# Nyström attention and two MLPs on one core: fewer products ahead of the first h, loads gated by VectorE, three f of chunk 0 split

## The chip, the cores and the metric

One NeuronCore of a Trainium2 chip runs the kernel. The metric is the device time of one execution in microseconds; the times before are three runs with a median of 875.27 us (874.94 to 875.64).

## The reference

Attention by landmarks over q, k, v of 4 batches, 8 heads, 576 positions, 64 wide, then a feed-forward layer with elu (512 to 2048 to 512), then a gated one with silu (512 to 1536 to 512). The MLP weights come as float64, and a part of the work is to turn their words into float32.

```python
q_lm = q.reshape(B, H, m, S // m, D).mean(axis=3)      # m = 32
k_lm = k.reshape(B, H, m, S // m, D).mean(axis=3)
A, Bm, C = sm(q, k_lm), sm(q_lm, k_lm), sm(q_lm, k)
Z = Bm.transpose(0, 1, 3, 2) / (norm_1(Bm) * norm_inf(Bm) + 1e-06)
for _ in range(6):
    Z = 2 * Z - Z @ Bm @ Z
x = A @ Z @ C @ v                                      # tokens 2304 x 512
h = x @ w_in
x = where(h > 0, h, exp(minimum(h, 0)) - 1) @ w_out
g = x @ w_gate
return silu(g) * (x @ w_val) @ w_out2
```

## The kernel before

The tokens are cut into chunks of 512 columns, four and a rest of 256. Attention goes batch by batch: batch 0 stands ahead of everything, batch b + 1 is woven into the MLP of chunk b. For a batch, `softmax_b`, `scores_c`, `softmax_c` and `cv` (lines 248 to 300) make the two small softmaxes and C v; `newton` (line 311) runs six steps on 32 x 32 blocks, eight heads side by side in the array, through `by_head` (line 302); `make_w` joins Z and C v; `make_u` multiplies that with blocks of w_in (i0 to i15), so that u times A gives h. `batch_a` makes A ("att"), from d, in pieces.

In a chunk, for each of 16 f, `h_mm` makes h, `elu` makes e and hl from it on ScalarE and VectorE, and two f later `y_mm` (line 521) adds hl times w_out (o0 to o15) to y. A "whole" y multiplies float32 as it is: 4 products of 512 columns. A split one takes both factors in a high and a low part in float32r: 12 products. In chunk 0, f below Y0 are whole; the later chunks are split throughout. `Weights` (line 121) prepares a weight in letters: W loads it through SP, S or s scales its upper words on ScalarE or POOL, B, D and E are three bit operations on VectorE, h, L and M split it. A load first needs a buffer ("raw") from the pool.

The order of all this is written out by hand: `PLAN` is a string of letters for the stretch ahead of chunk 0 and one for each chunk, and `play` (line 212) takes a step of the thread with that letter. Each engine and SP's queue work in that order. In PLAN[0], n is a newton step, C, c, v the C part, a and A steps of `batch_a` (with A, all of a step is on VectorE; with a, its subtraction and division are on POOL). `ps_start` (line 109) gives out the PSUM tiles ahead of the first h, and puts `BUSY[i]` products of zeros (bf16, 256 columns) into the i-th of them before its use; the list asks for 127 in all.

In a newton step of batches 0 and 1, the products with the identity add the old Z in PSUM, and ScalarE copies the tile out; from batch 2 on, VectorE adds it:

```python
if st["b"] < 2:
    if not last:
        by_head(pn, 64, rq[:, :, 0:32], rq[:, :, 0:32], 0)
    z = rq[:, :, 32:64]
    by_head(pn, 64, rq[:, :, 0:32], rq[:, :, 32:64], 32, plus=z)
```

Of the kernel before, what the change touches and what calls it, by code (L numbers as in the profile page):

```python
# [34 lines left out]
Y0, U0 = 16, 4  # L35
# [11 lines left out]
    "BEUDEWDEWSBSW,UBSWDEDE,,BDUS,qBEqD,,WSBEDWqESBlqUlWSW,BWlDWsEB,DWWWDEslB,WDESBSEW,,DbSBBsE,CDEBVDEs,DWVsn"
    "SBBW,UScEDDB,Ccn,DEEBEWs,DWnWBDSEEvBDSW,sBD,WnBW,EnWvnvSSDEBD,WBEDnEUsBE,AA,,vnAaaDEsB,Aa,hL,aAhAxD,,,E,x"
    "wu,L",
    "hUqqqL,U,l,,l,lqhLl,,bn,,Vn,hCMhM,,c,VnhChc,LhMn,,MnvhMh,,Lvvn,,UhLhLn,,v,aa,hM,A,haanAa,,M,AA,h,wMaxux,",  # L50
    "qqq,,,llU,,,l,,,q,l,b,Ccn,Un,,,VvCc,V,nU,v,vn,A,a,n,an,a,aaan,,Av,,An,Axx,xwxu",
    "U,U,WUWSs,BDWEWBD,hSE,MWhW,BDEL,hSBD,EW,hMSBDEM,WSh,WBSDEh,M,MsBDEhs,WBDE,hsW,LW,BDEBhDLE,hSMBDSW,EMWh,SB"
    ",DEMWhBS,MBWDE,shDE,WMhS,BDEM,BDW,EWhM,SB,WhX,MWsBDEhDE,,h",
    "SMSBDWSBDEhMEh,WSBDEhMWMSBDEh,MWBDEhMsB,WDEhMWSSBDEhMW,SBDEhMWBSDEhM,SBDEMWSBDEhWS,WhMBDEWhMMSBDE,WhSBDEM"
    "hS,BDEMBDEh,LWSBDhEhMM,,WSBDEhM",
# [13 lines left out]
def kernel(ctx: ExitStack, tc: tile.TileContext, qT, kT, va, vb, wi, wo, wg, wv, wo2, out):  # L69
# [232 lines left out]
    def by_head(p, width, a, b, o=0, plus=None):  # L302

        for g in range(2):
            q = slice(width * g + o, width * g + o + b.shape[2])
            for x, y in (((ident, plus),) if plus is not None else ()) + ((a, b),):
                for j in range(0, 128, 32):
                    PE.matmul(p[j:j + 32, q], lhsT=x[j:j + 32, j:j + 32] if x is ident else x[j:j + 32, g], rhs=y[j:j + 32, g],  # L308
                              start=plus is None or y is plus, stop=y is b, tile_position=(j, j), skip_group_check=True)
# [411 lines left out]
```

## Time and profile before

| what | value |
|---|---|
| median of three runs | 875.27 us |
| the profiled execution's own time | 876.06 us |
| its span, first to last instruction | 874.3 us |
| TensorE busy | 854.0 us, 98% |
| VectorE, ScalarE, POOL busy | 439.2, 323.0, 118.6 us |
| mean granted TensorE clock | 0.992 |
| DMA | 74.27 MB in 27997 packets |

The profiled execution is 0.8 us above the median, and 1.8 us of it lie outside the span. PE is TensorE (PEld its weight loads), DVE is VectorE, ACT is ScalarE, POOL is GpSimd, SP the queue from which DMAs are issued. A float32 product shows as two records of PE and two of PEld, a bf16 one as one of each.

### The profile page before, as it was taken

The numbers are of one execution on the slowest core, as the hardware profiler recorded it, in microseconds if no ns is written. First come the engines' busy times: TensorE is split into PE (matmuls) and PEld (weight loads), VectorE is DVE, ScalarE is ACT, GpSimd is POOL, SyncE is SP. The second block draws the span as 40 slices with busy tenths as digits, with TensorE's granted clock in tenths as the row PEclk, the third lists the DMA queues.
The fourth block names the chain that finished last, engine by engine and source line by source line (L and its number), as shares of the span: only waits on it lengthen the run. The fifth ranks groups of instructions, "written<-read, shape, count | busy, mean of one in ns | idle before, by whom it ended". The sixth has DMA issues, their size and how long they took to land.

```text
span 874.3 us, 13572 instructions
## 1 busy us (share of the span) xinstructions
PE 854.0 (98%) x5593; PEld 666.9 (76%) x5593; DVE 439.2 (50%) x788; ACT 323.0 (37%) x643; POOL 118.6 (14%) x111
## 2 busy tenths in 40 slices
PE   7899999999999999999999999999999999999998
PEld 5533445777787768999888888888888888888897
DVE  7598765634654367767578853222222223222332
ACT  3254436565656456666534322111111112111211
POOL 0120012334231315445100000000000000000000
PEclk9799999999999999999999999999999999999999
DMA  9990003300240025333480233000300001000100
GB/s 332 403 362 0 3 1 128 133 1 2 88 172 1 1 104 211 121 145 121 145 336 16 82 121 97 0 1 1 109 12 1 1 25 48 1 1 1 49 1 25
DMA packets 27997, 74.27 MB, mean 85 GB/s; under 512 B 3104, under 2 KB 5664, under 8 KB 27936
## 3 DMA queue, kind: packets, MB, share of 16 engines
q1 hardware_dynamic: 27936, 73.41, 23.3%
q8 instruction: 44, 0.72, 0.3%
q14 instruction: 17, 0.14, 0.1%
HBM read 59.24 MB, written 14.16 MB: 84 GB/s over the span
## 4 chain that ended last, share of the span: by engine, by line
PE 93%; ACT 3%; DMA 2%; issue 1%; DVE 1%; SPq 0%; DVEq 0%; ACTq 0%
PE ps_b L626 34%; PE ps_acc L642 17%; PE ps_acc L531 14%; PE ps_acc L526 6%; PE ps_b L501 6%; PE ps_b L491 3%; PE ps_b L531 3%; PE ps_b L495 3%; PE ps_b L407 1%; PE ps_b L245 1%; DMA raw<-wo 1%; PE ps_b L308 1%; DMA qk<-kT 1%; ACT us L192 1%; PE ps_b L294 1%
## 5 line engine op out<-in xcount | busy, mean ns | idle before, releaser
L626 PE MATMUL ps_b<-x,w 128*128 128x512 f32 (+1 forms) x1440 | 305.2, 368 | 0.0
L626 PEld LDWEIGHTS ps_b<-x,w 128*128 128x128 f32 x1440 | 252.3, 188 | 45.8
L642 PE MATMUL ps_acc<-w,hl 128*128 128x512 f32 x648 | 156.8, 389 | 0.0
L531 PE MATMUL ps_acc<-hl,w 128*128 128x512 f32 x576 | 141.0, 394 | 0.0
L642 PEld LDWEIGHTS ps_acc<-w,hl 128*128 128x128 f32 x648 | 120.9, 188 | 24.6
L531 PEld LDWEIGHTS ps_acc<-hl,w 128*128 128x128 f32 x576 | 106.0, 188 | 24.2 <-issue 2.3
L632 DVE TENSOR_TENSOR s<-s,ps_b 128x512 f32<-128x512 f32 (+1 forms) x60 | 38.0, 634 | 168.8 <-ACT s L631 168.8
L193 POOL TENSOR_TENSOR hl<-e,hl 128x512 fp32r<-128x512 f32 x64 | 80.5, 1267 | 169.9 <-ACT hl L192 161.7
L631 ACT ACTIVATE s<-ps_b 128x512 f32<-128x512 f32 (+1 forms) x60 | 33.2, 554 | 166.7 <-PE ps_b L626 166.7
L192 ACT ACTIVATE hl<-s 128x512 fp32r<-128x512 f32 (+1 forms) x60 | 35.4, 589 | 147.7 <-DVE s L633 147.7
L501 PE MATMUL ps_b<-xs,us 128*128 128x448 f32 (+3 forms) x384 | 75.1, 337 | 0.1
L510 DVE SCALAR_TENSOR_TENSOR e<-e,ps_b 128x512 f32<-128x512 f32 x64 | 39.4, 619 | 69.1 <-ACT e L508 66.7
L633 DVE TENSOR_TENSOR s<-s,ps_b 128x512 f32<-128x512 f32 (+1 forms) x60 | 38.0, 634 | 61.4 <-PE ps_b L626 60.4
L507 ACT ACTIVATE e<-ps_b 128x512 f32<-128x512 f32 x80 | 44.1, 552 | 61.5 <-PE ps_b L501 34.4
L501 PEld LDWEIGHTS ps_b<-xs,us 128*128 128x128 f32 x384 | 60.2, 189 | 1.8 <-DVE us L193 0.8
L193 DVE TENSOR_TENSOR hl<-s,hl 128x512 fp32r<-128x512 f32 (+1 forms) x60 | 38.3, 639 | 42.2 <-ACT hl L192 42.2
L526 PE MATMUL ps_acc<-hl,wf 128*128 128x512 f32 x128 | 58.0, 597 | 0.0
L168 DVE SCALAR_TENSOR_TENSOR wr<-raw,wr 128x512 int32<-128x512 int32 x68 | 50.6, 746 | 1.2
L508 ACT ACTIVATE e<-e 128x512 f32<-128x512 f32 x80 | 47.1, 589 | 2.5
L192 ACT ACTIVATE hl<-e 128x512 fp32r<-128x512 f32 x64 | 35.1, 573 | 28.9 <-DVE e L510 25.4
L526 PEld LDWEIGHTS ps_acc<-hl,wf 128*128 128x128 f32 x128 | 23.7, 190 | 28.8 <-issue 28.0
L183 ACT ACTIVATE w<-raw 128x512 fp32r<-128x512 f32 x36 | 24.1, 671 | 44.8 <-DVE raw L177 44.8
(142 smaller groups left out, 722.8 us busy)
## 6 DMA issues: line engine op xcount, KB each, us to landing
raw<-wo SPq DMA_DIRECT2D x28, 512.0 KB, 8.5
raw<-wi SPq DMA_DIRECT2D x16, 512.0 KB, 9.3
x<-x2d SPq DMA_DIRECT2D x16, 512.0 KB, 4.9
raw<-wg SPq DMA_DIRECT2D x12, 512.0 KB, 4.7
raw<-wv SPq DMA_DIRECT2D x12, 512.0 KB, 4.9
qk<-qT SPq DMA_DIRECT2D x16, 288.0 KB, 5.2
qk<-kT SPq DMA_DIRECT2D x16, 288.0 KB, 5.5
out<-o SPq DMA_DIRECT2D x18, 256.0 KB, 2.1
```

Source lines behind the costliest of these rows:

```text
L168: DVE.scalar_tensor_tensor(self.r[i], self.words(i)[1], -2 ** 31, self.r[i], ALU.bitwise_and, ALU.bitwise_or)
L192: ACT.activation(dst[:, 0], src, AF.Copy)
L193: (lo or DVE).tensor_tensor(dst[:, 1], src, dst[:, 0].bitcast(F32), ALU.subtract)
L501: PE.matmul(p[:, o:o + n], lhsT=state[b]["us", f // 4, g][:, a, cols], rhs=state["xs", c, g][:, b_, 0:n], start=i == 0, stop=i == 5)
L507: ACT.activation(e[:, 0:n], p[:, 0:n], AF.Relu, scale=-1.0)
L508: ACT.activation(e[:, 0:n], e[:, 0:n], AF.Exp, scale=-1.0)
L510: DVE.scalar_tensor_tensor(g[:, 0:n], e[:, 0:n], -1.0, p[:, 0:n], ALU.add, ALU.max)
L526: PE.matmul(acc[dc][:, 0:n], lhsT=w1.f[at1["o", f]][:, cols], rhs=g[:, 0:n], start=first, stop=last)
L531: PE.matmul(acc[dc][:, 0:n], lhsT=w[:, a, cols], rhs=g[:, b_, 0:n], start=first and i == 0 and (n == CH or dc % 2 == 0), stop=last and i = ...
L626: PE.matmul(p[:, 0:n], lhsT=w[:, a, 128 * kk:128 * kk + 128], rhs=x[kk][:, b_, 0:n], start=i == 0, stop=i == 11)
L632: DVE.tensor_tensor(s[:, 0:n], s[:, 0:n], pg[:, 0:n], ALU.mult)
L642: PE.matmul(acc[t], lhsT=u[:, a, 128 * t:128 * t + 128], rhs=w[:, b_], start=f == 0 and i == 0, stop=f == NF2 - 1 and i == 2)
```

## The change

The products of zeros become wide: float32, 512 columns, of a 128 x 128 tile of zeros with one column broadcast, and six in all are asked for. In batch 0 a newton step takes one identity product of 128 rows for all heads; batch 1 goes the way of batches 2 and 3. A new letter G writes one element of the next load's buffer on VectorE, so that this load, and all behind it on SP's queue, waits until VectorE has come to that place; it stands once in PLAN[0] and once in PLAN[1]. Y0 goes from 16 to 13, so that f = 13 to 15 of chunk 0 are split. All PLAN strings are others.

```diff
-Y0, U0 = 16, 4
+Y0, U0 = 13, 4
 PLAN = (
-    "qqqlqWlWVVlWlbSSAWAAnBBWCcCcDSnSvEAnDSaBAvAWnDnvABnAnnBDvWwEuEDSaEsB",
+    "qqqllqWSWlWVlbACacBnWWaDCsBSBnnavscsEnaaWvnVDaBAnGAvnnvWwBuDEEDAEsBSWs",
...
 BUSY = (
-    31, 0, 0, 0, 0, 0, 0, 0, 0, 0, 0, 15, 0, 15, 3, 0, 27, 0, 0, 0, 5, 4, 0, 17, 4, 0, 0, 0, 0, 0,
-    0, 0, 0, 0, 0, 0, 6,
+    3, 0, 0, 0, 0, 0, 0, 0, 0, 0, 0, 2, 0, 0, 0, 0, 0, 1, 0, 0, 0, 0, 0, 0, 0, 0, 0, 0, 0, 0,
+    0, 0, 0, 0, 0, 0, 0,
 )
...
-    zeros = const.tile([128, 256], BF16, name="zeros")
+    zeros = const.tile([128, 128], F32, name="zeros")
...
-            PE.matmul(p[:, 0:256], lhsT=zeros[:, 0:128], rhs=zeros, start=True, stop=True)
+            PE.matmul(p, lhsT=zeros, rhs=zeros[:, 0:1].to_broadcast([128, 512]), start=True, stop=True)
...
+                "G": self.gate(),
...
+        def buffer(self, i):
+            if i not in self.raw:
+                self.raw[i] = self.pools(i)[0].tile([128, 512], I64, tag="w", name="raw")
+            return self.raw[i]
+
         def load(self, i):
-            raw = self.raw[i] = self.pools(i)[0].tile([128, 512], I64, tag="w", name="raw")
-            SP.dma_start(raw, self.srcs[i])
+            SP.dma_start(self.buffer(i), self.srcs[i])
+            self.loaded = i + 1
+
+        def gate(self):
+
+            while True:
+                DVE.memset(self.buffer(self.loaded)[0:1, 0:1].bitcast(I32)[:, 0:1], 0)
+                yield
...
-            if st["b"] < 2:
+            if st["b"] == 0:
 
                 if not last:
                     by_head(pn, 64, rq[:, :, 0:32], rq[:, :, 0:32], 0)
-                z = rq[:, :, 32:64]
-                by_head(pn, 64, rq[:, :, 0:32], rq[:, :, 32:64], 32, plus=z)
+                PE.matmul(pn[:, 0:128].rearrange("p (g n) -> p g n", g=2)[:, :, 32:64], lhsT=ident, rhs=rq[:, :, 32:64],
+                          start=True, stop=False, skip_group_check=True)
+                by_head(pn, 64, rq[:, :, 0:32], rq[:, :, 32:64], 32, start=False)
```

What the new strings do to the order shows at three places. First TensorE in the second half of batch 0's Newton steps. Before, from the transposes of the second half of C (ec) to the fillers behind the next step (L308 are newton's products, nrq its tile):

```order
L284 MATMUL ps_b<-ident,ec 128x128 x4
L286 MATMUL ps_acc<-ident,ec 64x128
L308 MATMUL ps_b<-nrq 32x32 x8
L308 MATMUL ps_b<-nrq,ident 32x32 x4
L308 MATMUL ps_b<-nrq 32x32 x4
L308 MATMUL ps_b<-nrq,ident 32x32 x4
L308 MATMUL ps_b<-nrq 32x32 x4
L113 LDWEIGHTS zeros
L113 MATMUL ps_acc<-zeros 128x256
```

In the change, from the last product of zeros to the second half of C v (L319 and L362 are newton's, L307 is C v):

```order
L113 MATMUL ps_b<-zeros 128x512
L319 MATMUL ps_b<-nrq 32x32 x8
L362 MATMUL ps_b<-nrq,ident 128x2x32
L319 MATMUL ps_b<-nrq 32x32 x8
L297 MATMUL ps_acc<-ident,ec 128x128 x4
L299 MATMUL ps_b<-ident,ec 64x128
L319 MATMUL ps_acc<-nrq 32x32 x8
L362 MATMUL ps_acc<-nrq,ident 128x2x32
L319 MATMUL ps_acc<-nrq 32x32 x8
L362 MATMUL ps_b<-nrq,ident 128x2x32
L319 MATMUL ps_b<-nrq 32x32 x8
L307 MATMUL ps_acc<-v,ect 32x64 x16
```

Two identity rows of four products each became one row of one product, and no zeros stand between the fourth step and w.

Second, VectorE just ahead of nzt, which w needs. Before (L297 to L299 are C v's second half, L374 is nzt, L165, L168 and L177 the three bit operations of a weight, L471 the transposed half of att):

```order
L168 SCALAR_TENSOR_TENSOR wr<-raw,wr 128x512
L297 TENSOR_SCALAR den<-sc 128x1
L298 RECIPROCAL den<-den 128x1
L299 TENSOR_SCALAR cvn<-ps_acc,den,nrc 128x64
L374 TENSOR_TENSOR nzt<-nrq,mask_82 128x256
L177 SCALAR_TENSOR_TENSOR wf<-raw,wr 128x512 x2
L168 SCALAR_TENSOR_TENSOR wr<-raw,wr 128x512
L471 STREAM_TRANSPOSE att<-d 128x576
```

In the change (L162 is the gate's write, L310 to L312 and L386 are C v and nzt):

```order
L162 MEMSET raw 1x1
L483 STREAM_TRANSPOSE att<-d 128x576
L310 TENSOR_SCALAR den<-sc 128x1
L311 RECIPROCAL den<-den 128x1
L312 TENSOR_SCALAR cvn<-ps_acc,den,nrc 128x64
L386 TENSOR_TENSOR nzt<-nrq,mask_82 128x256
L178 TENSOR_SCALAR wr<-raw 128x512
L181 SCALAR_TENSOR_TENSOR wr<-raw,wr 128x512
L190 SCALAR_TENSOR_TENSOR wf<-raw,wr 128x512 x2
```

The gate stands ahead of the first half of att; the load that it holds is i4, the 19th on SP's queue.

Third, ScalarE from w's copy on. Before (L397 copies u, L161 scales a weight, L507 and L508 are elu):

```order
L381 ACTIVATE wt<-ps_b 128x128
L397 ACTIVATE u<-ps_acc 128x128
L397 ACTIVATE u<-ps_b 128x128
L161 ACTIVATE raw<-raw 128x512
L397 ACTIVATE u<-ps_acc 128x128
L397 ACTIVATE u<-ps_b 128x128
L161 ACTIVATE raw<-raw 128x512 x2
L507 ACTIVATE e<-ps_b 128x512
```

In the change (L409 copies u, L174 scales, L519 is elu):

```order
L393 ACTIVATE wt<-ps_b 128x128
L409 ACTIVATE u<-ps_acc 128x128
L409 ACTIVATE u<-ps_b 128x128
L174 ACTIVATE raw<-raw 128x512
L409 ACTIVATE u<-ps_acc 128x128
L409 ACTIVATE u<-ps_b 128x128
L409 ACTIVATE u<-ps_acc 128x128
L409 ACTIVATE u<-ps_b 128x128
L174 ACTIVATE raw<-raw 128x512 x2
L519 ACTIVATE e<-ps_b 128x512
```

The third block of u moved ahead of the first elu; the first scaling is of i4 and the next two are of i6 and i7, all behind the gate.

## Rows read from the trace of the kernel before

**Rows 1.** The page: busy time by engine; a DMA queue, packets, MB, share.

```profile
PE 854.0 (98%) x5593; PEld 666.9 (76%) x5593; DVE 439.2 (50%) x788; ACT 323.0 (37%) x643; POOL 118.6 (14%) x111
...
q8 instruction: 44, 0.72, 0.3%
```

**Rows 2.** Windows: us; busy us of PE, PEld, DVE, ACT, POOL; clock; DMA.

```profile
15.00:28.80 13.80, 11.14 (x267) 9.06 (x270) 13.23 (x35) 6.80 (x20) 1.85 (x2) 0.99 1.02 392
28.80:39.00 10.20, 7.72 (x187) 5.32 (x184) 3.23 (x9) 1.41 (x5) 0.00 (x0) 0.50 1.04 401
42.30:100.00 57.70, 56.19 (x346) 23.72 (x340) 52.47 (x106) 28.61 (x64) 5.29 (x7) 1.00 0.39 148
100.00:874.00 774.00, 766.34 (x4640) 620.39 (x4638) 358.33 (x613) 281.82 (x545) 109.12 (x90) 1.00 0.19 65
```

**Rows 3.** Chain of waits, 10 to 50 us: start us, us, what.

```profile
22.81 3.05 PE ps_acc L113 x27
...
26.17 1.45 issue
...
28.75 0.73 PE ps_b L308 x48
...
31.43 2.48 issue
...
35.78 1.38 PE ps_acc L294 x40
37.16 2.91 PE ps_b L113 x17
```

**Rows 4.** Timeline of TensorE: start us, us, engine, line, op, tiles, count.

```profile
40.90 0.29 PE L392 MATMUL ps_acc<-wf,wt 64*32 64x128 f32 x1
...
42.32 1.98 PE L491 MATMUL ps_b<-att,u 128*128 128x512 f32 x4
...
48.62 3.70 PE L526 MATMUL ps_acc<-hl,wf 128*128 128x512 f32 x8
...
92.23 0.33 PE L308 MATMUL ps_b<-nrq 32*32 32x32 f32 x16
...
92.78 0.66 PE L284 MATMUL ps_b<-ident,ec 128*128 128x128 f32 x4
...
177.49 0.43 PE L308 MATMUL ps_b<-nrq 32*32 32x64 f32 x16
177.85 1.17 PE L245 MATMUL ps_b<-qk,lc 64*32 64x288 f32 x16
```

**Rows 5.** Timeline of VectorE; in brackets its idle time before, and what ended it.

```profile
18.48 0.41 DVE L342 SCALAR_TENSOR_TENSOR nrq<-ps_acc,nnrc,eye 128x32 f32<-128x32 f32 x2
...
37.23 0.34 DVE L299 TENSOR_SCALAR cvn<-ps_acc,den,nrc 128x64 f32<-128x64 f32 x1 [6.93 <-PE ps_acc L294]
37.49 0.41 DVE L374 TENSOR_TENSOR nzt<-nrq,mask 128x256 f32<-128x256 f32 x1
```

**Rows 6.** Timeline of POOL.

```profile
21.64 1.20 POOL L456 TENSOR_TENSOR d<-d,amx 128x576 f32<-128x576 f32 x1 [19.74 <-DVE amx L455]
```

**Rows 7.** Timeline of ScalarE.

```profile
22.87 1.30 ACT L458 ACTIVATE d<-d 128x576 f32<-128x576 f32 x2 [0.65 <-POOL d L456]
24.07 0.26 ACT L360 ACTIVATE nrq<-ps_b 128x128 f32<-128x128 f32 x1
...
40.48 0.28 ACT L381 ACTIVATE wt<-ps_b 128x128 f32<-128x128 f32 x1 [4.35 <-PE ps_b L378]
```

**Rows 8.** Line 150, the loads of weights: from issue to landing.

```profile
DMA to landing us min/median/max: 3.4/8.0/11.5
```

**Rows 9.** Chain of waits of the whole span: a whole y, a split one.

```profile
54.04 3.43 PE ps_acc L526 x8
...
156.84 2.75 PE ps_acc L531 x12
```

More of the change, by code (lines that the diff above doesn't have):

```diff
@@ L45 @@
 PLAN = (
-    "qqqlqWlWVVlWlbSSAWAAnBBWCcCcDSnSvEAnDSaBAvAWnDnvABnAnnBDvWwEuEDSaEsB",
[L47 to L55, printed above, removed]
+    "qqqllqWSWlWVlbACacBnWWaDCsBSBnnavscsEnaaWvnVDaBAnGAvnnvWwBuDEEDAEsBSWs",
+    "DEWBUWDEUBSS,DED,B,WUqESB,DEGDE,q,lqWsWBBSDEDWqBUWEl,WsBllSWDEWBDW,WDESB,DEsBWWSBWS,EDEBSWD,bDEBE,WSDSWVB"
+    "VD,B,DSBSUWCEcDnWEEBE,SCcnWDBD,SEB,SsWBEDnESBSDWWvD,E,S,nvBDEnvEBDE,BU,haa,Dn,ESBDLvEaAha,A,ahnM,Aaa,n,,w"
+    "xxu,L,hh",
+    "hMULq,UM,lq,,lV,qqll,,ChLbn,,n,hhhM,,cnLM,Cc,Vnh,h,vhM,L,vnv,nLhL,hULhLn,,,ava,,Aa,anAA,Aa,A,,,wxxu,",
+    "q,,,lqUq,q,l,V,,lUl,,,bVn,Cc,n,,,nv,Cc,U,,n,A,a,n,vaAnA,v,AA,AAvn,,,n,Axwxxxu,",
+    "U,U,WWWS,WUBsWDBEhD,SE,LWBWh,WDEL,hsB,,sLDEh,WsBDM,BSEhLS,,BDEhDEs,WBDE,hhLWS,,BDEhBDLW,EhMSBMD,EhMWW,,SB"
+    "DEhssMB,,DEWM,WBSWWDES,BS,WW,DE,,,BDBDE,,hWESXhhhWBDELM",
+    "WWhhMSLMsBDSBDEhMSE,BBSDMEWhM,DEBhMhMDEh,sBDEhWMSSBDWS,EhBDEhWWMBDEM,hMSsBDMEWBWSDEshM,WhMWBDEhMSBDE,WhSB"
+    "DBEhLMWs,DEBDh,SBDEhEMhMM,,WSBDEhL",
 )
 BUSY = (
-    31, 0, 0, 0, 0, 0, 0, 0, 0, 0, 0, 15, 0, 15, 3, 0, 27, 0, 0, 0, 5, 4, 0, 17, 4, 0, 0, 0, 0, 0,
-    0, 0, 0, 0, 0, 0, 6,
+    3, 0, 0, 0, 0, 0, 0, 0, 0, 0, 0, 2, 0, 0, 0, 0, 0, 1, 0, 0, 0, 0, 0, 0, 0, 0, 0, 0, 0, 0,
+    0, 0, 0, 0, 0, 0, 0,
 )
@@ L129, in __init__ @@
             self.splits = splits
+            self.loaded = 0
             n = range(len(srcs))
@@ L300, in cv, with by_head @@
         yield
-    def by_head(p, width, a, b, o=0, plus=None):
+    def by_head(p, width, a, b, o=0, start=True):
         for g in range(2):
[L305 to L309, printed above, removed]
+            for j in range(0, 128, 32):
+                PE.matmul(p[j:j + 32, width * g + o:width * g + o + b.shape[2]], lhsT=a[j:j + 32, g], rhs=b[j:j + 32, g],
+                          start=start, stop=True, tile_position=(j, j), skip_group_check=True)
     def newton(st, ps):
@@ L357, in newton @@
             rn = at.tile([128, 2, 64], F32, tag="nrq", bufs=2, name="nrq")
-            if st["b"] < 2:
+            if st["b"] == 0:
                 o = 32 if last else 0
```

## The prediction

> **What bounds the kernel now.** I read the page first. TensorE is busy for 854.0 us of a span of 874.3, and it runs 5593 matmul records and as many weight loads [rows 1]. So the time falls only if TensorE gets less to do or stands less. Then the windows, to see where it stands. From 100 us to the end it idles 774.0 − 766.34 = 7.7 us, and from 42.3 to 100 it idles 1.5 us [rows 2]. Ahead of that, 854.0 − 56.19 − 766.34 = 31.5 us of 42.3 are busy, so some 11 are idle, and much of the busy time is filler. The loss is at the front, so the front's chain of waits comes next [rows 3]: the filler of 27 products takes 3.05 us of the chain and that of 17 takes 2.91, and twice TensorE waits for nothing that the profile shows, 1.45 and 2.48 us, each time in the middle of a Newton step. The timeline of TensorE then gives the marks by which I count: the first product of u at 40.90, the first h at 42.32, the first y at 48.62 [rows 4]. From there on the other engines have to keep ahead of it; VectorE is the nearest to failing, with 52.47 us of work in the 57.7 us from 42.3 to 100 [rows 2].
>
> The two unnamed waits I read as instructions that have not arrived. Queue 8 moved 44 packets of instructions [rows 1], 2 × 5593 / 44 = 254 instructions each, and both waits fall where the DMA share is 1.02 to 1.04 [rows 2], that is, where no DMA engine has room. The Trainium skill's page "Runtime: NRT & Kernel Launch", section "Instruction fetch mechanics", also gives 256 instructions to a block; it says besides that crossing into a new block is mostly hidden. By that sentence the waits would be something else and would stay; that case is a rival below, worked out from the two rows.
>
> **The change part by part.**
>
> *Fewer instructions ahead of the first h.* A small float32 product is two weight loads and two matmuls, a filler one of each. Six steps with 8 identity products give 192 instructions; as one wide product each, 24. The fillers go from 127 × 2 = 254 to 6 × 4 = 24. Some 400 instructions are gone, about one and a half packets, and loads pause besides. I take both waits as gone: −3.9 us of the chain, bounds 0 and −3.9. The wide product (128 by 64 columns) has no row; below it is nothing, above it stand the four records of w's two products, 0.4 us at half clock; the eight that it replaces cost about 0.2. I book nothing.
>
> *Newton's chain, walked through the new orders.* The first step begins when VectorE has written rq, which ended at 18.9 [rows 5]; one weight row moves behind it, so about 18.5. The third copy now waits for both exponentials of d, and both subtractions ahead of them are on POOL, one behind the other. Before, one was there: 1.20 us from 21.64 [rows 6], the two exponentials began at 22.87 and the second step's copy ended at 24.33 [rows 7]. Now the second subtraction ends near 24.05, its exponential (0.65) near 24.7, and the copy at 25.0, but this is the third step's copy. From there no filler of length is left. Three steps at 0.73 us at half clock [rows 3], a copy of 0.26 each [rows 7] and some 0.1 us for a handover make 3.3 us, to 28.3; the last products of v 1.38 [rows 3], to 29.7; cvn and nzt 0.34 + 0.41 [rows 5], less their overlap, to about 30.3; w's products and their copy (0.28, [rows 7]) to 31.0. The first product of u thus starts near 31.0 where it started at 40.90, 9.9 us earlier: 3.9 of unnamed waits, some 6 of filler and waiting behind it.
>
> *The gate.* The write of one element costs VectorE 0.1 to 0.2 us, twice. It stands behind both sums of d and both divisions, which wait for the exponential at 24.7: about 27.9. Every load behind it on SP waits, batch 1's q and k too. A weight load lands 3.4 us after issue at the least [rows 8]: i4 near 31.4, with the 8.0 median of a full queue as the other bound; the queue is empty then, so I take 3.4. ScalarE scales i4 ahead of the copies of u's second block, so these end near 32.9, the third block follows, and the first h starts at about 33.4 instead of 42.32. The second gate stands behind the third hl, near 45.6; o3 lands near 49 and its y is wanted near 58. That wait is covered by the products of f = 0 to 2.
>
> *The clock.* It was 0.50 (1.2 GHz) from 28.8 to 39.0 and 1.00 (2.4 GHz) afterwards, so the first h found it up [rows 2], after the last filler. Now TensorE comes to h from short products with gaps between. Three h of four records each at 3.43 / 8 us [rows 9] and the last of u are about 5.4 us at full clock. Bounds of the loss: nothing, if it is up at once; 2.6 us if it stays down for 5.1 us, as long as it did between the end of the second unnamed wait at 33.9 and 39.0. That row is the nearest thing, and part of that stretch was loose work, so I take 2.0. The first y: 33.4 + 5.4 + 2.0 = 40.8, against 48.62: **−7.8 us**. ScalarE scales i6 and i7 before the first e; at 392 GB/s [rows 2] they land 2.6 and 3.9 us after i4, so e begins near 36 and hl of f = 0 is there some 2 us later, in time. The Trainium skill, page "TensorE: Matmul & The Clock Gate", section "What's actually happening", says the throttled state is the default and activity releases it, which speaks against taking the filler out; the trace agrees that the clock was down while TensorE stood and up after the filler, and the rule's own outcome is the slow rival below.
>
> *Three f split.* A whole y is 3.43 us of TensorE, a split one 2.75 [rows 9]: 3 × 0.68 = **−2.0 us**. The splitting of those three weights is only earlier; the three extra splits of g cost ScalarE and POOL about a us each, under TensorE's stream, since they have two f of lead.
>
> *Newton of batch 1.* A step took 92.78 − 92.23 = 0.55 us; one without identity takes 177.85 − 177.49 = 0.36 [rows 4]. Six steps: **−1.1 us**. VectorE gains six short additions.
>
> *VectorE.* Its second transposed attention block is done about 6.7 us earlier, TensorE wants things 7.8 us earlier, and it had 5.2 us idle from 42.3 to 100 [rows 2]. Most of the lag fits; I book **+0.5 us**, bounds 0 and +3.
>
> Sum: −7.8 − 2.0 − 1.1 + 0.5 = −10.4. The profiled execution took 876.06 us, so 865.7; the median before is 0.8 below it, so **864.9 us**.
>
> **The rivals.**
>
> *The waits stay.* If the two unnamed waits are not fetching, or fetching still collides with loads, 3.9 us come back: 868.8. For it: the 18 loads ahead of the gate, 6.7 MB, keep the DMA engines full to about 21 at 392 GB/s [rows 2]. Against: counted along the order (four instructions to a small float32 product, two to a filler), the waits came some 700 and 970 instructions in; now the last Newton step and the first y lie there, when those loads have landed. Chance 0.13.
>
> *VectorE becomes the bound.* In chunk 0 it must prepare 26 weights and take part in batch 1's attention; if its lag of 1 us and the 4 us of paused loads can't be absorbed, TensorE waits for u's blocks or hl, 2 to 4 us: 867 to 869. For it: 91% busy. Against: hl has two f of lead, some 5 us. Chance 0.18.
>
> *The clock stays down (slower than before).* Without filler TensorE could run chunk 0 at 1.2 GHz. Each us at half clock loses half a us. My sum allows 4 us from 33.4; to eat the other 10.4 it must stay down 21 us more, to about 58. Staying to 65 gives about 879. For it: the clock was down for 10 us while TensorE was 76% busy [rows 2]. Against: wide products without a gap come from 33.4, and with such work it never fell after 39. Chance 0.04.
>
> *The front doesn't move.* If the chain from 18 to 31 is held by a wait that I have not seen (a late v, POOL's scalings ahead of the subtractions), only the last two terms remain, −3.1: 872.2, and a little more slowness makes it the same. Chance 0.06.
>
> **How the numbers follow.** My forecast has 0.59 and its own range is 862 to 868; the low end is a clock that is up at once and no lag of VectorE. The range for 8 in 10, 861.5 to 870.5, takes in the first two rivals and leaves out the last two. A measurement here can tell 0.2%, 1.75 us, from no change: the median must fall below 873.5. All cases but the last two do: faster 0.91; the same 0.05 (part of the last rival); slower 0.04.
>
> **What would show it.** First u product near 31, first h near 33.4, first y near 41; no unnamed wait of over 0.5 us on TensorE before the first h; a granted clock of 0.5 around 25 to 37 and 1.0 after; no DMA from about 22 to 28; y of f = 13 to 15 at 2.75 us; batch 1's steps at 0.36. Wrong if the first y is later than 44, if TensorE idles over 3 us between the first y and 100 us, or if the clock is down beyond 45.

## The result, and the profile after

The changed kernel takes **864.6 us** in the median of four runs (863.06 to 866.53), against 875.14 for the kernel before (874.94 to 875.64): 0.988 of it, 95% interval 0.986 to 0.990. The prediction was 864.9. The profiled run took 864.63 with a span of 862.8. So the time came out as forecast, but the two halves of the sum did not: the front gave less than booked and the rest gave more.

The page of the changed kernel, to set against [rows 1]:

```profile
PE 847.2 (98%) x5236; PEld 659.7 (76%) x5236; DVE 434.3 (50%) x791; ACT 323.2 (37%) x641; POOL 131.9 (15%) x123
...
PEclk7899999999999999999999999999999999999999
...
q8 instruction: 41, 0.67, 0.3%
```

TensorE has 6.8 us less work, and three packets of instructions fewer came. Its windows (columns as in [rows 2]), cut where the granted clock changes:

```profile
10.30:20.40 10.10, 9.39 (x102) 4.14 (x104) 8.15 (x29) 2.98 (x11) 1.99 (x3) 0.50 0.98 376
20.50:34.10 13.60, 10.71 (x312) 7.27 (x302) 12.91 (x30) 5.94 (x19) 3.33 (x3) 1.00 0.29 92
34.20:40.90 6.70, 5.73 (x22) 2.57 (x23) 5.06 (x9) 3.92 (x9) 1.16 (x1) 0.50 1.03 405
45.00:100.00 55.00, 54.23 (x301) 23.65 (x299) 50.34 (x110) 27.20 (x60) 3.30 (x4) 1.00 0.61 233
100.00:862.00 762.00, 757.03 (x4469) 618.10 (x4468) 348.21 (x601) 279.23 (x537) 120.95 (x101) 1.00 0.19 66
```

By these rows the clock was at 1.2 GHz twice: for ten us while the scores of C and the first Newton products ran, and for seven while the last of u and the first three h ran. TensorE's timeline has the marks that answer to [rows 4]:

```profile
18.36 1.91 PE L113 MATMUL ps_b<-zeros 128*128 128x512 f32 x2
20.21 0.41 PE L319 MATMUL ps_b<-nrq 32*32 32x32 f32 x16
...
32.30 0.29 PE L404 MATMUL ps_acc<-wf,wt 64*32 64x128 f32 x1 [0.37 <-ACT wt L393]
...
35.17 0.42 PE L404 MATMUL ps_acc<-wf,wt 64*32 64x128 f32 x1 [1.39 <-ACT u L409]
...
35.95 7.89 PE L503 MATMUL ps_b<-att,u 128*128 128x512 f32 x12
...
44.14 3.70 PE L538 MATMUL ps_acc<-hl,wf 128*128 128x512 f32 x8
...
86.60 0.42 PE L319 MATMUL ps_b<-nrq 32*32 32x64 f32 x16
86.96 0.66 PE L297 MATMUL ps_b<-ident,ec 128*128 128x128 f32 x4
```

And the chain of waits, 10 to 50 us, shows what held the first h, where [rows 3] had fillers and waits without a name:

```profile
19.43 0.41 DVE nrq L353 x2
...
29.30 4.97 DMA raw<-wi
34.30 0.67 ACT raw L174
34.96 0.17 ACT u L409
```

First u product 32.30 (before 40.90), first h 35.95 (42.32), first y 44.14 (48.62). Between the first y and the end of TensorE's work lay 870.49 − 48.62 = 821.9 us before and 858.98 − 44.14 = 814.8 now. So of the 11.5 us between the two spans **4.5 came from ahead of the first y and 7.0 from behind it**; 7.8 and 2.6 were forecast. These two lengths are what the experiments are judged by. For the table, the half clock is read from short windows of the profile, its ends to about half a us; "rest" is first y to the end of TensorE's work; all are of the profiled run, whose own time stands last.

| kernel | first h | first y | rest | at 1.2 GHz | us |
|---|---|---|---|---|---|
| before | 42.32 | 48.62 | 821.9 | 12–15, 29–39 | 876.06 |
| changed | 35.95 | 44.14 | 814.8 | 10–20.5, 34–41 | 864.63 |
| no gate | 35.55 | 42.57 | 815.2 | 11–21, 35–38 | 863.49 |
| i4 ahead of the gate | 39.66 | 47.88 | 814.9 | 11–14, 21–44.5 | 868.37 |
| no zeros | 39.07 | 46.56 | 815.6 | to 15, 19–42.5 | 867.80 |
| one zero more, at w | 40.78 | 48.87 | 815.1 | 11.5–14.5, 22–45.5 | 869.61 |
| Y0 = 16 | 36.08 | 43.84 | 816.9 | 9.5–16, 33.5–40 | 866.35 |
| identity in batch 1 | 36.47 | 44.33 | 817.6 | 10–20, 34–40.5 | 867.66 |
| before, no zeros | 36.52 | 45.09 | 821.6 | to 14, 17.5–41.5 | 872.31 |
| old order of chunk 2 | 35.51 | 44.00 | 817.8 | 10.5–20.5, 34–41 | 867.45 |
| zeros at more places | 33.92 | 39.64 | 815.2 | never after 8 | 860.47 |
| the same, no gate | 36.89 | 42.61 | 815.2 | 28–35 | 863.43 |
| the same, i4 behind | 36.24 | 41.97 | 814.9 | 27.5–34.5 | 862.52 |
| small identity | 35.15 | 43.58 | 815.7 | 10–20, 30.5–40.5 | 864.88 |

The clock at the very start needs care: until some 5 to 8 us (14 and 15 us in the two kernels without zeros) the profile reads 1.00, but the products run at half that pace. TensorE's timeline of the kernel with zeros at more places has the same twelve records of zeros before and after:

```profile
1.91 5.49 PE L113 MATMUL ps_acc<-zeros 128*128 128x256 f32 x12 [1.91 <-DVE zeros L107]
...
15.50 2.88 PE L113 MATMUL ps_b<-zeros 128*128 128x256 f32 x12
```

And 16 records of scores have a pitch of 0.96 us at 12.9 in the run without zeros, 0.49 at 12.4 here. So I count the start as 1.2 GHz; the table says so only where it reaches beyond 8 us.

In every row the time is first y + rest + 5.6, to 0.1 us. Where the code of the chunks is the changed kernel's, the rest stays within 814.8 to 815.7, whatever the front does; so one profile's difference in the rest is good to about 0.9 us. Of the 7.0 us, 4.1 are less work of TensorE behind the first y (816.2 to 812.1 us busy) and 2.9 less idle time (5.7 to 2.7).

### The profile page after: what moved, and what is told of

It is laid out like the page before. It is cut to its first block, busy times and chain, and to the rows that moved or that the text cites. A ratio compares the mean times of both kernels' runs of the same rounds, so it can differ in the third digit from the quotient of the medians.

```text
span 862.8 us, 12887 instructions
## 1 busy us (share of the span) xinstructions
PE 847.2 (98%) x5236; PEld 659.7 (76%) x5236; DVE 434.3 (50%) x791; ACT 323.2 (37%) x641; POOL 131.9 (15%) x123
## 4 chain that ended last, share of the span: by engine, by line
PE 95%; DVE 2%; DMA 1%; ACT 1%; issue 0%; SPq 0%; DVEq 0%
PE ps_b L638 34%; PE ps_acc L654 17%; PE ps_acc L543 17%; PE ps_b L513 7%; PE ps_acc L538 5%; PE ps_b L503 4%; PE ps_b L507 3%; PE ps_b L543 3%; PE ps_b L419 2%; PE ps_b L258 1%; PE ps_b L319 1%; DMA qk<-kT 1%; DMA raw<-wi 1%; PE ps_b L307 1%; DVE lc L244 0%; PE ps_b L297 0%
## 5 line engine op out<-in xcount | busy, mean ns | idle before, releaser
L543 PE MATMUL ps_acc<-hl,w 128*128 128x512 f32 x612 | 151.1, 396 | 0.0
L543 PEld LDWEIGHTS ps_acc<-hl,w 128*128 128x128 f32 x612 | 112.3, 188 | 28.2 <-issue 3.3
L206 POOL TENSOR_TENSOR hl<-e,hl 128x512 fp32r<-128x512 f32 (+1 forms) x67 | 83.2, 1252 | 179.0 <-ACT hl L205 167.6
L522 DVE SCALAR_TENSOR_TENSOR e<-e,ps_b 128x512 f32<-128x512 f32 (+1 forms) x67 | 41.4, 621 | 89.4 <-ACT e L520 85.7
L519 ACT ACTIVATE e<-ps_b 128x512 f32<-128x512 f32 x80 | 44.1, 552 | 66.5 <-PE ps_b L513 39.6
L181 DVE SCALAR_TENSOR_TENSOR wr<-raw,wr 128x512 int32<-128x512 int32 x68 | 52.4, 773 | 1.1
L205 ACT ACTIVATE hl<-e 128x512 fp32r<-128x512 f32 (+1 forms) x67 | 37.0, 575 | 30.9 <-DVE e L522 29.0
L538 PE MATMUL ps_acc<-hl,wf 128*128 128x512 f32 x104 | 47.3, 597 | 0.0
L196 ACT ACTIVATE w<-raw 128x512 fp32r<-128x512 f32 x36 | 23.8, 670 | 42.4 <-DVE raw L190 40.5
L538 PEld LDWEIGHTS ps_acc<-hl,wf 128*128 128x128 f32 x104 | 19.3, 190 | 23.2 <-issue 22.3
```

Of the source, the lines that this page charges most:

```text
L181: DVE.scalar_tensor_tensor(self.r[i], self.words(i)[1], -2 ** 31, self.r[i], ALU.bitwise_and, ALU.bitwise_or)
L205: ACT.activation(dst[:, 0], src, AF.Copy)
L206: (lo or DVE).tensor_tensor(dst[:, 1], src, dst[:, 0].bitcast(F32), ALU.subtract)
L519: ACT.activation(e[:, 0:n], p[:, 0:n], AF.Relu, scale=-1.0)
L522: DVE.scalar_tensor_tensor(g[:, 0:n], e[:, 0:n], -1.0, p[:, 0:n], ALU.add, ALU.max)
L538: PE.matmul(acc[dc][:, 0:n], lhsT=w1.f[at1["o", f]][:, cols], rhs=g[:, 0:n], start=first, stop=last)
```

## Experiments on the front

**No gate.**

```diff
-    "qqqllqWSWlWVlbACacBnWWaDCsBSBnnavscsEnaaWvnVDaBAnGAvnnvWwBuDEEDAEsBSWs",
-    "DEWBUWDEUBSS,DED,B,WUqESB,DEGDE,q,lqWsWBBSDEDWqBUWEl,WsBllSWDEWBDW,WDESB,DEsBWWSBWS,EDEBSWD,bDEBE,WSDSWVB"
+    "qqqllqWSWlWVlbACacBnWWaDCsBSBnnavscsEnaaWvnVDaBAnAvnnvWwBuDEEDAEsBSWs",
+    "DEWBUWDEUBSS,DED,B,WUqESB,DEDE,q,lqWsWBBSDEDWqBUWEl,WsBllSWDEWBDW,WDESB,DEsBWWSBWS,EDEBSWD,bDEBE,WSDSWVB"
```

> The changed kernel with both of VectorE's gates taken out of the order, so that no load waits; all products as in the changed kernel. Theory 1 (the unnamed waits of 1.45 and 2.48 us in the kernel before came from blocks of instructions that were fetched while the DMA engines were full, and it is the pause of the loads that removed them): an unnamed wait of 1 to 2.5 us comes back on TensorE between 24 and 36 us, the wait of 1.39 us for the scaling of i4 goes, and the first y starts between 44 and 46 (changed kernel: 44.14); time 864 to 867. Theory 2 (the smaller number of instructions alone removed them, because the block that the chain needs is fetched earlier): no unnamed wait over 0.5 us, i4 has landed by 25, the first h starts near 34.5 and the first y near 42.7; time 862.5 to 864. In both VectorE does the same work but for two short writes.

Measured: 865.34 us (863.49 to 867.37), 0.9885 of before (0.986 to 0.991). TensorE has no wait without a name between 18 and 40 us, though the loads never paused (DMA share 1.02 to 1.04 in each of the windows that cover 15 to 45). First y 42.57. That is theory 2 for the waits and the first y (the median lies above its range), and in this kernel the gate is not what removed the waits. The time is no better than that of the changed kernel within its spread.

**The kernel before, without zeros.**

```diff
 BUSY = (
-    31, 0, 0, 0, 0, 0, 0, 0, 0, 0, 0, 15, 0, 15, 3, 0, 27, 0, 0, 0, 5, 4, 0, 17, 4, 0, 0, 0, 0, 0,
-    0, 0, 0, 0, 0, 0, 6,
 )
```

> The kernel before, without any of its 127 small products of zeros, with nothing else changed. Theory 1 (the filler's only work is to hold the clock up, and without it the 192 identity instructions a step remain, with loads running): TensorE has the clock at 0.5 from some 20 us to 40 or later, the chain of small products takes longer, unnamed waits of 1 to 2.5 us stay since the loads still fill the DMA engines; first h 40 to 43, first y 48 to 50; time 873 to 877. Theory 2 (the filler is what makes the front long and also what pushes the instruction blocks over the full queue; taking it out is the whole gain of the front): no unnamed wait over 0.5, first y at 43 to 46; time 869 to 872. The stretch from the first y to the end of TensorE's work stays at 821.9 in both.

(The 192 identity instructions are those of all six steps, 32 a step.) Measured: 872.32 us (871.19 to 872.77), 0.9963 of before (0.995 to 0.998): 3 us faster, between the theories. TensorE ran at 1.2 GHz to 14 and from 17.5 to 41.5, and still the first y came 3.5 us earlier than with 127 fillers. The waits without a name shrank from 1.45 + 2.48 to these two in TensorE's timeline:

```profile
22.39 0.28 PE L305 MATMUL ps_b<-nrq,ident 32*32 32x32 f32 x5 [0.36 <-issue]
...
34.92 0.37 PE L389 MATMUL ps_acc<-wf,wt 64*32 64x128 f32 x1 [0.61 <-issue]
```

With 254 instructions fewer 3.0 of 3.9 us are gone while the loads run on at a DMA share of 1.03; with the identity's instructions gone as well (no gate, above) all are. (Its chain also runs at half clock, which leaves a late block more time; the run without gate has full clock from 21 to 35.) So with few enough instructions ahead of the first h these waits are gone, and the pause of the loads is not needed for it. That what is late are blocks of instructions stays an inference: queue 8 moved 44, 43 and 41 packets in the three kernels. The Trainium skill, page "Runtime: NRT & Kernel Launch", section "Instruction fetch mechanics", says that crossing into a new block is mostly hidden. If the waits are such crossings, the traces agree for the changed kernel (none is seen), while the kernel before has 3.9 us that were not hidden.

**Small identity.** The opposite edit in the changed kernel: the identity of batch 0's steps as eight products again.

```diff
-                PE.matmul(pn[:, 0:128].rearrange("p (g n) -> p g n", g=2)[:, :, 32:64], lhsT=ident, rhs=rq[:, :, 32:64],
-                          start=True, stop=False, skip_group_check=True)
+                for g in range(2):
+                    for j in range(0, 128, 32):
+                        PE.matmul(pn[j:j + 32, 64 * g + 32:64 * g + 64], lhsT=ident[j:j + 32, j:j + 32], rhs=rq[j:j + 32, g, 32:64],
+                                  start=True, stop=False, tile_position=(j, j), skip_group_check=True)
```

> The changed kernel with the identity of batch 0's six Newton steps again as eight small products (32 by 32), which brings back 168 of TensorE's instructions ahead of the first h; zeros, gate and order stay. Judged by the unnamed waits and by the first y (44.14 in the changed kernel, 42.6 in the run without gate). Theory 1 (it is the number of instructions that the blocks have to bring, and the first gate frees the DMA engines for them): no unnamed wait over 0.5 us; a step is 0.05 to 0.25 us shorter at full clock, since eight small products have a pitch of 0.1 to 0.2 where the wide one has 0.37; first y 0.3 to 1.2 us earlier where the clock runs as in the changed kernel. Theory 2 (the wide product was needed): an unnamed wait of 0.6 to 2.5 us between 20 and 36 us.

The output of this kernel is another than the reference's (I take it because all identity products of a step begin their sums ahead of all others, so that z of batch 0 differs; no run tests it). So it stands for instructions and waits alone, which are those described. Measured: 865.06 us (two runs), 0.988 of before (0.986 to 0.990). No wait without a name, first h 0.8 us earlier than in the changed kernel, first y 0.6. So theory 1: the wide product was not needed for that. The small ones gain little: the first u product starts 0.3 us earlier (32.03), since TensorE waits 1.51 us for VectorE's nzt (0.89 in the changed kernel); the rest of the 0.8 goes with i4, which landed after 3.5 us here and 4.97 there.

This run also limits what was shown of the pause. The traces have 1231 records of TensorE (products and weight loads) ahead of the first h in the kernel before, 989 without its zeros, 1045 here, 877 in the changed kernel with or without gate. Here, with the loads paused (DMA share 0.02 from 20.5 to 29), 1045 records run without an unnamed wait; with loads running and in the old order, 989 still have 0.97 us of them. At that number the pause, or the order, may count; no run takes the two apart.

**No zeros in the changed kernel.**

```diff
 BUSY = (
-    3, 0, 0, 0, 0, 0, 0, 0, 0, 0, 0, 2, 0, 0, 0, 0, 0, 1, 0, 0, 0, 0, 0, 0, 0, 0, 0, 0, 0, 0,
-    0, 0, 0, 0, 0, 0, 0,
 )
```

> The changed kernel without any of its six wide products of zeros. Theory 1 (those six hold the clock up from 20.5 to 34.1, and without them Newton's steps and w run at 1.2 GHz): granted clock 0.5 from some 10 us to 37 or later, first h 1 to 3 us later than 35.95, the three h of f = 0 to 2 at half clock for longer than in the changed kernel, first y 46 to 48; time 866 to 868.5. Theory 2 (they only fill time, and the chain of copies between the steps sets the pace): the first h comes 0 to 1.5 us earlier, first y 43 to 44.5; time 863 to 865.

Measured: 867.35 us (866.49 to 867.80), 0.990 of before (0.9885 to 0.991); first h 39.07, first y 46.56. Theory 1 in the times. The clock rises for a short stretch at 15, falls at 19 while TensorE stands for nrq (3.27 us, to 19.79), and stays at 1.2 GHz until 42.5; the three h take 7.2 us, not more than in the changed kernel.

**i4 ahead of the gate, and one zero more.** Two edits that should each take something off the front.

```diff
-    "qqqllqWSWlWVlbACacBnWWaDCsBSBnnavscsEnaaWvnVDaBAnGAvnnvWwBuDEEDAEsBSWs",
+    "qqqllqWSWlWVlbACacBnWWaDCsBSBnnavscsEnaaWvnVDaBAnWGAvnnvwBuDEEDAEsBSWs",
```

> The changed kernel with the load of i4 moved ahead of the first gate, so that the gate holds back i5 and what follows. Theory 1 (after the fix of the chain it is i4's landing, 4.97 us behind the gate where 3.4 was booked, that sets the first h): i4 lands before 26, the wait of 1.39 us on TensorE for the scaled u goes, the first h starts near 34.5 instead of 35.95 and the first y 1.4 to 2.5 us earlier than 44.14; time 862 to 863.5. Theory 2 (the copies of u and the scaling queue on ScalarE is what h waits for): the first h moves by less than 0.5 us, and the time stays within 1 us of the changed kernel's 864.6.

```diff
-    3, 0, 0, 0, 0, 0, 0, 0, 0, 0, 0, 2, 0, 0, 0, 0, 0, 1, 0, 0, 0, 0, 0, 0, 0, 0, 0, 0, 0, 0,
+    3, 0, 0, 0, 0, 0, 0, 0, 0, 0, 0, 2, 0, 0, 0, 0, 0, 1, 0, 0, 0, 0, 0, 1, 0, 0, 0, 0, 0, 0,
```

> The changed kernel with one more wide product of zeros, ahead of the products of w, where TensorE stands for about 0.9 us. Theory 1 (the fall of the clock to 0.5 at 34.1 comes from the thin work between 29 and 34, and costs 2.7 us, the three h taking 7.8 us where twelve records at full clock take 5.15): the clock stays at 1.0 through the three h, they take 5.2 to 6, the first y is 1.5 to 2.7 us earlier than 44.14; time 862 to 863.5. Theory 2 (one product is too little, or what decides is the wait of 1.39 us ahead of the first h): the clock falls as before, the first y stays within 0.6 us; time 864 to 865.5.

With i4 ahead, both theories missed; with one zero more, two runs lie in theory 1's range of time and two above both. This is the finding. With i4 ahead, all four runs took 867.08 to 868.97 (0.991, 0.9896 to 0.9925): TensorE did not wait for i4, but was at 1.2 GHz from 21 to 44.5. With one zero more the four runs took **862.77, 862.80, 869.58 and 869.61** (0.989, 0.9845 to 0.993), at a mean granted clock of 0.995 to 0.996 in the first two and 0.982 to 0.984 in the others. Its profile is of a long one; the short ones have no trace:

```profile
11.40:14.50 3.10, 3.10 (x52) 1.78 (x60) 1.76 (x6) 1.20 (x5) 0.66 (x1) 0.51 1.05 405
14.70:21.60 6.90, 4.89 (x83) 2.62 (x67) 6.43 (x25) 2.05 (x7) 1.28 (x2) 0.99 0.83 309
22.00:45.00 23.00, 21.34 (x290) 12.03 (x285) 16.20 (x34) 8.28 (x26) 3.97 (x4) 0.50 0.51 193
```

(windows, columns as before). In the changed kernel's own profile the clock was down while the zeros ahead of the first step ran, took 3.7 us over four records, and came up at 20.5 for the small products. Here it was up for them, they were done in 2 us, TensorE stood for nrq for 1.17 us (in the run with i4 ahead for 1.35), and the clock fell for all that followed. I infer that the stands at 7 to 11 and 15 to 20 us decide which stretch the slow clock hits; the next run tests it by filling them. Between the runs of this one kernel the difference is 6.8 us.

**Zeros at more places.** So zeros of half the width were put where TensorE stands: after each of the first three pairs of landmarks' products, ahead of nbt's, more of them ahead of the first step, and at w and the first u; with i4 ahead of the gate.

```diff
-    3, 0, 0, 0, 0, 0, 0, 0, 0, 0, 0, 2, 0, 0, 0, 0, 0, 1, 0, 0, 0, 0, 0, 0, 0, 0, 0, 0, 0, 0,
+    6, 0, 0, 0, 0, 0, 0, 0, 0, 0, 1, 6, 0, 0, 0, 0, 0, 2, 0, 0, 0, 0, 0, 2, 1, 0, 0, 0, 0, 0,
...
-            PE.matmul(p, lhsT=zeros, rhs=zeros[:, 0:1].to_broadcast([128, 512]), start=True, stop=True)
+            PE.matmul(p[:, 0:256], lhsT=zeros, rhs=zeros[:, 0:1].to_broadcast([128, 256]), start=True, stop=True)
...
+            if st["b"] == 0 and pr < 3:
+                PE.matmul(pb[1][:, 256:512], lhsT=zeros, rhs=zeros[:, 0:1].to_broadcast([128, 256]), start=True, stop=True,
+                          skip_group_check=True)
```

> The changed kernel with the load of i4 ahead of the first gate, and with the zeros as products of half the width (256 columns) at more places: six ahead of everything as before in work, one after each of the first three pairs of landmarks' products, one ahead of the first of Newton's products, six (in place of four) ahead of the first step, two at w, one at the first u. Theory 1 (the front of the changed kernel swings by up to 5 us, first y at 42.6 to 48.9 in the runs so far, because the waits at 7 to 11, 15 to 16 and 18 to 20 us let the clock fall at a moment that differs from run to run; filled, it stays up): granted clock 1.0 from some 12 us to the end of the front or at half for at most one stretch of 3.5 us, first h at 34 to 35, first y at 39.8 to 42, time 860 to 862.5, and the runs lie within 2.5 us of each other. Theory 2 (such filler cannot hold the clock, or at half clock it delays the chain itself): first y at 44 or later, runs from 863 to 870.

Measured: **860.68 us** (860.03 to 863.39), 0.984 of before (0.982 to 0.985). Theory 1, but for the spread, which one of five runs makes 3.4 us. Its windows and marks on TensorE:

```profile
10.00:20.00 10.00, 8.63 (x142) 5.82 (x142) 9.12 (x32) 3.27 (x12) 1.73 (x3) 1.00 1.03 393
20.00:31.00 11.00, 9.64 (x256) 7.01 (x255) 10.32 (x24) 4.97 (x17) 3.58 (x4) 1.00 0.32 105
31.00:45.00 14.00, 13.18 (x91) 5.82 (x92) 13.83 (x27) 7.88 (x19) 1.67 (x1) 1.00 0.64 238
```

```profile
18.62 0.42 PE L322 MATMUL ps_b<-nrq 32*32 32x32 f32 x16 [0.24 <-DVE nrq L356]
...
33.92 5.42 PE L506 MATMUL ps_b<-att,u 128*128 128x512 f32 x12
...
39.64 3.70 PE L541 MATMUL ps_acc<-hl,wf 128*128 128x512 f32 x8
```

The first step starts 1.6 us earlier than in the changed kernel, and the twelve records of h take 5.4 us, not 7.9. This is faster than both kernels. The Trainium skill, page "TensorE: Matmul & The Clock Gate", section "What's actually happening", says that the throttled state is the default and activity releases it. The trace agrees in that the first zeros run at half pace and the clock is up from 8 us on, behind them.

Two variants of it. First without either gate, with i4 in its place of the changed kernel:

> The same as the run with zeros at more places, but with both of VectorE's gates taken out and i4 where the changed kernel has it, so that no load ever waits. Theory 1 (with so few instructions TensorE never waits for a block, full DMA engines or not, and the gate gives nothing): no unnamed wait over 0.5 us, first y within 0.6 us of the kernel with the gate wherever the clock ran alike, and the median within 1.5 us of it. Theory 2 (the gate is worth something: without it a block of instructions or a later load is late): an unnamed wait of over 0.5 us in the front, or waits for weights after the first y; 1.5 to 4 us slower.

Measured: 859.99 us (859.70 to 863.43), 0.983 of before (0.981 to 0.985), no wait without a name from 20 to 40 us: theory 1 on the gate (the first y, 42.61, can't be compared, since the clock ran differently). The profiled run was the longest of the four; its clock fell at 28 for seven us, when TensorE had stood 0.76 and 0.46 us for nrq. Those two stands alone don't decide it, for TensorE's timeline of the run with the gate has them too, and there the clock stayed up:

```profile
24.98 0.33 PE L322 MATMUL ps_b<-nrq 32*32 32x32 f32 x16 [0.76 <-ACT nrq L375]
...
27.96 0.43 PE L365 MATMUL ps_b<-nrq,ident 128*128 128x64 f32 x2 [0.46 <-ACT nrq L375]
```

Then with the gate, i4 behind it:

> The kernel with zeros at more places (860.68 us, first y 39.64), but with the load of i4 back behind the first gate, where the changed kernel has it; so the two differ in the place of one load. Theory 1 (behind the gate the landing of i4 is what the first h waits for, whatever the clock does): a wait of 1 to 3 us on TensorE for u, since the chain before it is some 1.5 us earlier than in the changed kernel while the gate moves less; first h 35 to 36.5 in place of 33.92, first y 41 to 42, or 43 to 44 where that wait lets the clock fall; time 862 to 864.5. Theory 2 (the clock was all, i4 only waits because the clock makes the rest late): first h within 0.6 us of 33.92, time within 0.8 us of 860.7.

Measured: 861.98 us (859.89 to 862.56), 0.984 of before (0.9825 to 0.985). The 1.3 us between the medians fit theory 1, but the spreads overlap, and in the profiled run the slow clock (27.5 to 34.5) delayed u so far that nothing waited for i4. Of the runs at a mean clock of 0.999 to 1.000, those with i4 behind took 859.89, 861.97, 861.98 and 862.56, those with i4 ahead 860.03 to 860.77; so its place seems to be worth 1 to 2 us in most runs, but none of these slower ones was traced, and through what it acts stays open.

Of the fourteen runs of these three kernels, eleven have a mean clock of 0.999 or 1.000 (859.70 to 862.56 us) and three one of 0.996 (862.52 to 863.43). So the zeros hold the clock in most runs, not in all.

## Experiments on the rest

**Y0 back to 16.**

```diff
-Y0, U0 = 13, 4
+Y0, U0 = 16, 4
```

> The changed kernel with Y0 back at 16, so that the last three f of chunk 0 run whole instead of split; the order is otherwise that of the change. Judged by the stretch from the first y to the end of TensorE's work, which took 814.8 us in the changed kernel's profile (44.14 to 858.98) and 814.2 to 815.2 in the runs before this one, while the front moves with the clock. Theory 1 (the three split f give 3 x 0.68 = 2.0 us, the term of the prediction): the stretch gets 2.0 us longer, 816.8. Theory 2 (part of the -7.0 us that this stretch lost is more than that, since the split work also moves what follows): 3 us or more. Theory 3 (the splits cost elsewhere what they give): under 1 us.

(By the table, the runs ahead of this one had a rest of 814.9 to 815.6.) Measured: rest 816.95, 2.1 us longer: theory 1, though the rest alone spreads by 0.9. (Time 866.35 us, 864.17 to 870.97, 0.990 of before, 0.987 to 0.994; the front's clock makes the spread.)

**Identity in batch 1.**

```diff
-            if st["b"] == 0:
+            if st["b"] < 2:
```

(in both places)

> The changed kernel with the wide identity product and the copies on ScalarE also in the six Newton steps of batch 1, as batch 0 has them, in place of VectorE's six additions. Judged by the stretch from the first y to the end of TensorE's work, 814.8 us in the changed kernel. Theory 1 (the identity's cost on TensorE is all there is): a wide product has a pitch of 0.37 us at full clock, six of them make the stretch 2.2 us longer; the eight small ones of the kernel before cost 1.1. Theory 2 (VectorE's additions there delay the weights it prepares, and without them TensorE waits less): 1 us or less.

Measured: rest 817.63, 2.8 us longer; 868.79 us (two runs), 0.9925 of before (0.990 to 0.9945). Theory 1, with 0.6 more than booked, because a step now has two sets of products of 32 columns where it had one of 64. TensorE's timeline has one of its steps:

```profile
96.95 0.33 PE L319 MATMUL ps_b<-nrq 32*32 32x32 f32 x16
97.20 0.43 PE L362 MATMUL ps_b<-nrq,ident 128*128 128x64 f32 x2
97.57 0.33 PE L319 MATMUL ps_b<-nrq 32*32 32x32 f32 x16
97.83 0.65 PE L307 MATMUL ps_b<-v,ect 128*32 128x64 f32 x32
```

The wide product has a pitch of 0.37 us, and the whole step takes 97.83 − 96.95 = 0.88. With eight small products a step of the kernel before takes 0.55, without identity 0.36 [rows 4]. So the wide one adds 0.52 to a step and the eight small ones 0.19: it has fewer instructions and takes longer. No run puts the eight small ones back into batch 1.

**The old order of chunk 2.**

```diff
-    "q,,,lqUq,q,l,V,,lUl,,,bVn,Cc,n,,,nv,Cc,U,,n,A,a,n,vaAnA,v,AA,AAvn,,,n,Axwxxxu,",
+    "qqq,,,llU,,,l,,,q,l,b,Ccn,Un,,,VvCc,V,nU,v,vn,A,a,n,an,a,aaan,,Av,,An,Axx,xwxu",
```

> The changed kernel with the order of work of chunk 2 (one string of the plan, in which batch 3's landmarks, Newton steps, w and first u are placed) put back to that of the kernel before. Judged by the stretch from the first y to the end of TensorE's work, 814.8 us in the changed kernel. Theory 1 (part of what that stretch gained, and which the prediction did not name, is that w and the first u of batch 3 now stand a whole y earlier, so that VectorE's split of u is covered): waits for us on VectorE of 0.5 to 1.1 us come back at the end of chunk 2, near 306 to 320, 1.8 to 2.6 us in all, 816.6 to 817.4. Theory 2 (those waits went because VectorE has less work or lags less): under 0.7 us.

Measured: rest 817.78, **2.9 us longer**, a little above theory 1; 867.57 us (two runs), 0.991 of before (0.989 to 0.993). The waits are back, the same as in the kernel before. TensorE's timeline at the end of chunk 2, of the kernel before:

```profile
320.08 0.92 PE L495 MATMUL ps_b<-att,u 128*128 128x192 f32 x4 [0.60 <-DVE us L193]
...
323.66 1.68 PE L407 MATMUL ps_b<-wf,wt 64*32 64x512 f32 x16 [1.08 <-DVE us L193]
```

and of this run:

```profile
311.22 0.92 PE L507 MATMUL ps_b<-att,u 128*128 128x192 f32 x4 [0.60 <-DVE us L206]
...
314.81 1.68 PE L419 MATMUL ps_b<-wf,wt 64*32 64x512 f32 x16 [1.08 <-DVE us L206]
```

In the changed kernel a y of 12 records stands between the first and the second part of u there:

```profile
305.43 1.10 PE L419 MATMUL ps_b<-wf,wt 64*32 64x256 f32 x32 [0.38 <-ACT wt L393]
306.46 3.01 PE L543 MATMUL ps_acc<-hl,w 128*128 128x512 f32 x12
309.40 1.09 PE L419 MATMUL ps_b<-wf,wt 64*32 64x512 f32 x16
```

Under those 3 us VectorE splits u (307.25 to 308.54). Of the 2.9 us, the two waits make 1.7, and the 16 records of u behind the longer one, 1.68 us where the changed kernel takes 1.09, another 0.6; the rest was not taken apart. In the plan it is the ending: w and the first u's part stand one unit ahead of the last (`Axwxxxu,` for `Axx,xwxu`; other letters of the string differ too, and the swap took them along).

## Why the prediction was right, and where not

The total was right because two errors met, and that was luck. The sum had −7.8 for the front and −2.6 for the rest; the runs showed −4.5 and −7.0. Of the 3.3 us that the front fell short, 2.55 stand ahead of the first h (35.95 for 33.4) and 0.8 behind it.

- **"Both waits as gone: −3.9 us of the chain."** They are gone, and the reason given first, the count of instructions, is enough for that in the changed kernel; the pause of the loads, given beside it, is not needed there. The rival that the waits stay fell. ("Some 400 instructions are gone": the traces have 354 records fewer.)
- **"So about 18.5", the first Newton step.** It began at 20.21. The scores of C ran at 1.2 GHz from 10 us on, so VectorE wrote rq only at 19.43 to 19.84, and the zeros ahead of the step, at half clock too, ran to 20.27. The prediction looked at the clock from 25 us on only, though the kernel before also had a short fall at 12. With zeros at more places and the clock up, the step began at 18.62 and the third copy ended at 24.94, where 25.0 was forecast; so the walk along the chain was right to there but for the clock. Of the 1.7 us, 1.3 came through: first u product 32.30 for 31.0, gate at 29.21 for 27.9.
- **"The queue is empty then, so I take 3.4", i4's landing.** It took 4.97 us in the profiled run. The wait that this made, 1.39 us ahead of the last part of u, is the longest on TensorE between 11 us and the first h. What made it long is open. The loads that follow it on the queue do not explain it: with the same loads behind the same gate, i4 landed after 3.5 to 3.7 us in five traces (no zeros, one zero more, small identity, old order of chunk 2, zeros at more places with i4 behind) and after 5.3 and 5.5 in two (Y0 = 16, identity in batch 1). The bounds, 3.4 and 8.0, held it.
- **"I take 2.0", the half clock in the three h.** 7.9 us for twelve records where 5.4 are enough, 2.5 lost; the bound of 2.6 was nearer. The place was right, the stretch (34 to 41) later and shorter than the 25 to 37 forecast: in this run the clock was up from 20.5 to 34. Without zeros it was down from 19 to 42.5, but with the same zeros and i4 ahead it was down from 21 to 44.5, so that too was partly luck. The whole front thus ended at 44.14; by its own mark, "wrong if the first y is later than 44", this part of the forecast failed.
- **"Three f split: −2.0."** Measured alone, 2.1, to within 0.9.
- **"Newton of batch 1: −1.1."** A step takes 86.96 − 86.60 = 0.36 us, as forecast; the sum over six steps was not measured alone.
- **"+0.5 us" for VectorE's lag.** None shows: from 45 to 100 TensorE idles 0.8 us, nearly all of it one wait of 0.77 for u, which the kernel before has too. This is where the failed step of the rest lies: the prediction looked in the new order for what could be late, and put at nothing the waits of the old one that could go. They were in the 7.7 us that it had read from the window of 100 to the end, of which 3.5 lie behind the last product (870.49) and 4.2 between products. The new end of chunk 2 gives 2.9. With 2.0 and 1.1 that makes 6.0 of 7.0. The other 1.0 is hardly more than the spread of the rest; this wait for u in TensorE's timeline, which only the kernel before has, would be most of it, but no run took it apart:

```profile
83.60 1.98 PE L491 MATMUL ps_b<-att,u 128*128 128x512 f32 x4 [0.74 <-ACT u L413]
```

- **The clock stays down** (the slow rival). Part of it is real: the front has half-clock stretches that differ from trace to trace, and runs of one kernel lie up to 6.8 us apart, the slower ones at the lower mean clock. Its price, 14 us, was far off: once the wide products of h and y run without a gap, the clock came up in every profiled run, at 45.5 at the latest.

## What to carry to other kernels

Judge a change by stretches that do not touch each other: here the time is first y + rest, and a median that agrees with the forecast hid errors of 3.3 and 4.4 us of opposite sign. Try filler for the clock where TensorE would stand anyway, and in a few wide products, and judge it by several runs: here 127 small ones cost 3 us net; six wide ones gave some 2.7 against none and left the rest to chance; more of them in the gaps gave 4 us more and a full clock in eleven of fourteen runs. Width and place of the filler were not tested apart. When an order is replaced, list the waits of the old order first, each one by place, and ask of each whether the new order covers it.

## What was not expected of the hardware

The same kernel on the same chip took 862.8 twice and 869.6 twice, with nothing on record but the mean granted clock to tell them apart (0.995 or 0.996, and 0.982 or 0.984). Zeros that ran at half clock (3.8 us, in the changed kernel) went with full clock for the chain behind them, zeros that ran at full clock (2.0 us, with i4 ahead and with one zero more) with half clock; that the gap they left made it fall is an inference. One wide identity product of 128 rows adds 0.52 us to a Newton step, eight of 32 rows together 0.19. The first load of 512 KB behind a pause of the queue landed after 3.5 to 5.5 us with the same loads behind it, where the shortest landing of the kernel before is 3.4 [rows 8]. And the clock that the profile reads ahead of its first change is no measurement: 1.00, while the products ran at half pace.
